# Linear attention on one core: how the rows of two late output stores are dealt to DMA queues and engines

## The chip, the cores and the metric

The kernel runs on one core of a Trainium2 chip. The time is the device time of one execution in microseconds. The profile is one execution recorded by the hardware; its engines are PE (matmul; PEld its weight loads), DVE, ACT (ScalarE), POOL and SP, which issues DMAs, beside 16 DMA engines that move the data.

## The reference

Linear attention with the feature map elu + 1, for 32 heads, 2048 positions and 128 features in bf16:

```python
phi_q = jnp.where(q > 0, q + 1, jnp.exp(q)) + 1e-6
phi_k = jnp.where(k > 0, k + 1, jnp.exp(k)) + 1e-6
kv = jnp.einsum("bhsd,bhse->bhde", phi_k, v)
z = jnp.einsum("bhsd->bhd", phi_k)
num = jnp.einsum("bhqd,bhde->bhqe", phi_q, kv)
den = jnp.einsum("bhqd,bhd->bhq", phi_q, z)[..., None] + 1e-6
return num / den
```

Each head reads three arrays of 512 KB and writes one of 512 KB.

## The kernel before

A head is one unit of work. Its 2048 positions lie 16 to a partition, so a head of k, v, q or of the output is 128 rows of 4096 contiguous bytes, one row for each partition. For each head:

- SP issues three loads (L361) into a ring of six buffers.
- ACT takes exp of k (L368), DVE takes min(exp, 1) + eps (L382), POOL takes relu of k (L372) and adds both for some of the tiles (L390).
- PE accumulates phi_k times (1, v) in PSUM (L413); ACT copies the result to `kvs_sb` (L430).
- PE transposes q (L436); ACT takes exp of it (L447) and relu of one half (L454), DVE relu of the other half (L456) and min(exp, 1) + eps (L468).
- PE multiplies by `kvs_sb` (L483, L484); DVE takes denominators (L506), reciprocals (L512) and the products that are the output (L517, L524). For the last two heads ACT does some of these products (L536).
- SP issues the store (L571) from a ring of ten output buffers `o_sb`.

The order is written by hand. Every operation is added to a plan with an engine and a key (`pl.add`), and each engine runs its operations in order of their keys; the plan derives the semaphore waits from what an operation reads and writes. A DMA is issued by the engine in whose order it stands, and each engine that issues DMAs has a queue of its own. Loads have keys some six heads ahead; a store's key is `late = h + 1.0 + 0.18 * h`, so the stores fall behind the loads and the last ones come after all loads. Before the change all loads and stores are on SP's queue; ACT issues one DMA of 64 bytes at the very start.

A store adds to a semaphore of its slot: `bo`, the output buffer's number, for all heads, and slot `NBO` for the second part of the last head. At the end SP waits for all of them (L226).

`PARTS` (L252) names heads whose store is cut by partitions. Before the change it cuts head 29 (`LAST - 2`) into 51, 13 and 64 rows, all from SP, one behind the other. Head 30 goes out whole, head 31 in two parts by columns (2304 and 1792 bytes of each row).

On ACT the keys around the change are 29.05 for the copy of head 30's sums (L430), 29.9 for the exp of head 31's q (L447), the last exp of the kernel, and 30.0 for its relu (L454).

Of the kernel before, what the change touches and what calls it, by code (L numbers as in the profile page):

```python
# [7 lines left out]
P = 128  # L8
# [223 lines left out]
def bass_standalone__linear_attn_elu__prompt_kernel(  # L232
# [6 lines left out]
    B, H, S, D = q.shape  # L239
    assert D == P and S == 16 * P  # L240
    NT = 16
# [3 lines left out]
    NBI = 6  # L245
    NBO = 10
# [2 lines left out]
    NG = 7  # L249
    HALF = NT * P // 2  # L250
    LAST = NH - 1
    PARTS = {LAST - 2: (51, 13, 64)}  # L252

    ADD = (10, 11, 12, 13, 14)
    EVEN, ODD = tuple(range(0, NT, 2)), tuple(range(1, NT, 2))
# [7 lines left out]
    of = out.rearrange("b h s d -> (b h) s d")  # L263

    with ExitStack() as es:
        def sb(name, shape, dt):
            return es.enter_context(nc.sbuf_tensor(name, shape, dt))
# [13 lines left out]
        o_sb = sb("o_sb", [P, NBO, NT, D], bf16)  # L281
# [12 lines left out]
        def dma_sem(name):  # L294
            return dsems[name]

        for n, c in (("k", NBI), ("q", NBI), ("v", NBI), ("va", 1), ("o", NBO + 1)):
            for i in range(c):
                dsems[(n, i)] = es.enter_context(nc.semaphore(f"s_{n}{i}"))

        pl = Plan()

        def rows(x, h):
            return x[h].rearrange("(p j) d -> p (j d)", j=NT)
# [46 lines left out]
        for h in range(NH):  # L351
# [3 lines left out]
            bi, b2, b3, bo = h % NBI, h % 2, h % 3, h % NBO  # L355
# [211 lines left out]
                last_tile(h + 0.925)  # L567
                div(4, 5, h + 0.93)

            def store(t0, t1, key, parts, slot, p0=0, p1=P, h=h, bo=bo):  # L570
                pl.add("sp", key, lambda sp: sp.dma_start(rows(of, h)[p0:p1, t0 * D:t1 * D],  # L571
                                                          o_sb[p0:p1, bo, t0:t1].rearrange("p j d -> p (j d)")),
                       reads=[("o", bo, p) for p in parts], dma=("o", slot))

            late = h + 1.0 + 0.18 * h
            if h < LAST:
                p0 = 0
                for n in PARTS.get(h, (P,)):
                    store(0, NT, late, ("t", 0, 1, 2, 3, 4), bo, p0, p0 + n)
                    p0 += n  # L580
                assert p0 == P
            else:
                store(0, 9, late, (0, 1, 2), bo)
                store(9, NT, late + 0.01, (3, 4, "t"), NBO)
# [30 lines left out]
```

## Time and profile before

| | us |
|---|---|
| median of three runs (lowest, highest) | 168.23 (168.01, 168.49) |
| the profiled execution, its own time | 167.82 |
| its span | 166.5 |
| busy: PE, DVE, ACT, POOL | 156.0, 152.3, 155.0, 106.3 |
| DMA: 67.25 MB | mean 404 GB/s |
| SP's final wait for stores, in total | 3.0 |

The span runs from the first to the last recorded instruction; the time of an execution has some 1.3 us more around it. Busy times overlap, since engines work side by side: three engines over 90% busy do not say which one sets the end. For this, one reads the chain of waits back from the end, and near the end what the DMA engines still have to move. "To landing" is the time from the issue of a transfer until the last of its DMA engines has reported.

### The profile page before, as it was taken

The page shows a single profiled execution, that of the slowest core. Times are in us where ns is not written, and L with a number is a line of the kernel's source. Part 1 is how long each engine was busy: PE and PEld are TensorE (multiplying, and loading weights), DVE is VectorE, ACT ScalarE, POOL GpSimd, SP SyncE. Part 2 cuts the span into 40 slices and gives each one's busy share as a digit, 9 for nine tenths or more (in the row PEclk, how much of TensorE's full clock was granted, in tenths as well). Part 3 has the DMA queues.
Part 4 walks back from the last instruction along what each step waited for, and adds up shares of the span by engine and source line. Part 5 has one row for each costly group of instructions (what it writes and reads, how often), then busy time and mean ns, then how long its engine had stood idle before and what let it go on. Part 6 is the DMA issues. An engine that isn't in the chain of part 4 may idle for free.

```text
span 166.5 us, 6269 instructions
## 1 busy us (share of the span) xinstructions
PE 156.0 (94%) x2819; PEld 145.3 (87%) x2453; DVE 152.3 (91%) x270; ACT 155.0 (93%) x143; POOL 106.3 (64%) x128
## 2 busy tenths in 40 slices
PE   7789999999999999999999999999999999999960
PEld 0259999999999999899999989999998999999950
DVE  0587999999999999999999999999999999999991
ACT  3979999999999999999999999999999999998790
POOL 2405788676767877676778867676787767677300
PEclk9999999999999999999999999999999999999998
DMA  5999999999999999999999999999999999999986
GB/s 205 345 417 421 413 415 419 412 407 418 417 416 419 422 417 417 422 421 411 424 420 414 423 421 415 419 421 415 422 420 416 422 421 418 418 421 418 415 310 239
DMA packets 18605, 67.25 MB, mean 404 GB/s; under 512 B 2082, under 2 KB 2210, under 8 KB 18594
## 3 DMA queue, kind: packets, MB, share of 16 engines
q1 hardware_dynamic: 18592, 67.12, 99.4%
q8 instruction: 5, 0.08, 0.2%
q14 instruction: 6, 0.05, 0.1%
q10 hardware_dynamic: 2, 0.00, 0.0%
HBM read 50.33 MB, written 16.78 MB: 403 GB/s over the span
## 4 chain that ended last, share of the span: by engine, by line
DVE 58%; PE 17%; POOL 12%; ACT 6%; issue 3%; DMA 2%; DVEq 0%
DVE o_sb L524 20%; POOL rk_sb L390 12%; DVE rq_sb L456 11%; DVE emk_sb L382 10%; DVE emq_sb L468 9%; PE kvz_ps L413 6%; PE o_ps L483 5%; PE o_ps L484 5%; ACT ek_sb L368 3%; DVE rden_sb L512 3%; DVE o_sb L517 3%; ACT eq_sb L447 2%; DMA k_sb<-in_k_dram 2%; DVE den_sb L506 2%; DVE rk_sb L390 1%
## 5 line engine op out<-in xcount | busy, mean ns | idle before, releaser
L413 PE MATMUL kvz_ps<-v_sb,rk_sb 128*128 128x129 bf16 (+1 forms) x512 | 67.0, 220 | 2.8 <-DVE rk_sb L390 1.0
L524 DVE TENSOR_TENSOR o_sb<-o_ps,rden_sb 128x768 bf16<-128x768 f32 (+2 forms) x62 | 67.8, 1135 | 0.0
L390 POOL TENSOR_TENSOR rk_sb<-rk_sb,emk_sb 128x640 bf16<-128x640 bf16 x30 | 41.9, 1395 | 39.5 <-DVE emq_sb L468 38.2
L372 POOL TENSOR_SCALAR rk_sb<-k_sb 128x1024 bf16<-128x1024 bf16 (+1 forms) x60 | 64.1, 1068 | 2.5 <-DMA k_sb<-in_k_dram 2.5
L483 PE MATMUL o_ps<-kvs_sb,emq_sb 128*128 128x129 bf16 (+1 forms) x536 | 65.2, 217 | 0.0
L484 PE MATMUL o_ps<-kvs_sb,rq_sb 128*128 128x129 bf16 (+1 forms) x536 | 64.4, 217 | 0.0
L368 ACT ACTIVATE ek_sb<-k_sb 128x2048 bf16<-128x2048 bf16 x32 | 61.0, 1907 | 2.6 <-DMA k_sb<-in_k_dram 2.6
L447 ACT ACTIVATE eq_sb<-xT_ps 128x2048 bf16<-128x2048 bf16 (+1 forms) x33 | 60.0, 1821 | 2.0 <-PE xT_ps L436 2.0
L413 PE MATMUL kvz_ps<-v_sb,emk_sb 128*128 128x129 bf16 (+1 forms) x338 | 53.3, 221 | 0.6 <-DVE emk_sb L382 0.3
L413 PEld LDWEIGHTS kvz_ps<-v_sb,rk_sb 128*128 128x128 bf16 x512 | 46.1, 98 | 7.6 <-POOL rk_sb L390 2.7
L483 PEld LDWEIGHTS o_ps<-kvs_sb,emq_sb 128*128 128x128 bf16 x536 | 51.2, 98 | 0.8 <-issue 0.3
L484 PEld LDWEIGHTS o_ps<-kvs_sb,rq_sb 128*128 128x128 bf16 x536 | 51.3, 98 | 0.0
L436 PE MATMUL xT_ps<-ident,q_sb 128*128 128x128 bf16 x512 | 33.8, 219 | 0.6 <-DMA q_sb<-in_q_dram 0.4
L436 PEld LDWEIGHTS xT_ps<-ident,q_sb 128*128 128x128 bf16 x512 | 29.9, 98 | 5.1 <-DMA q_sb<-in_q_dram 4.2
L413 PEld LDWEIGHTS kvz_ps<-v_sb,emk_sb 128*128 128x128 bf16 x338 | 32.5, 98 | 0.9 <-DVE emk_sb L382 0.5
L320 PE MATMUL kvz_ps<-ones_sb,rk_sb 128*128 128x1 bf16 x232 | 31.3, 165 | 0.0
L454 ACT ACTIVATE rq_sb<-xT_ps 128x1024 bf16<-128x1024 bf16 x30 | 30.9, 1029 | 0.0
L382 DVE TENSOR_SCALAR emk_sb<-ek_sb 128x2048 bf16<-128x2048 bf16 x32 | 22.0, 688 | 5.6 <-ACT ek_sb L368 5.6
L456 DVE TENSOR_SCALAR rq_sb<-xT_ps 128x1024 bf16<-128x1024 bf16 x34 | 23.3, 690 | 1.1 <-PE o_ps L484 1.0
L468 DVE TENSOR_SCALAR emq_sb<-eq_sb 128x2048 bf16<-128x2048 bf16 x32 | 22.1, 690 | 0.0
L320 PE MATMUL kvz_ps<-ones_sb,emk_sb 128*128 128x1 bf16 x121 | 19.9, 166 | 0.0
L430 ACT ACTIVATE kvs_sb<-kvz_ps 128x129 bf16<-128x129 f32 x32 | 9.0, 281 | 1.6 <-PE kvz_ps L413 0.9
(28 smaller groups left out, 49.2 us busy)
## 6 DMA issues: line engine op xcount, KB each, us to landing
k_sb<-in_k_dram SPq DMA_DIRECT2D x32, 512.0 KB, 15.0
q_sb<-in_q_dram SPq DMA_DIRECT2D x32, 512.0 KB, 15.1
v_sb<-in_v_dram SPq DMA_DIRECT2D x32, 512.0 KB, 15.1
out_dram<-o_sb SPq DMA_DIRECT2D x30, 512.0 KB, 15.3
out_dram<-o_sb SPq DMA_DIRECT2D x1, 288.0 KB, 3.7
out_dram<-o_sb SPq DMA_DIRECT2D x1, 256.0 KB
out_dram<-o_sb SPq DMA_DIRECT2D x1, 224.0 KB, 3.6
out_dram<-o_sb SPq DMA_DIRECT2D x1, 204.0 KB
```

The source lines that it names most:

```text
L320: return pe.add_instruction(mybir.InstMatmult(start_tensor_calc=start, stop_tensor_calc=stop, ldweights=False, bass_skip_group_check=True, ...
L368: lambda a, bi=bi, b2=b2: a.activation(ek_sb[:, b2, :], k_sb[:, bi, :], ACT.Exp),
L372: pl.add(eng, key, lambda e: e.tensor_scalar(rk_sb[:, b3, c], k_sb[:, bi, c], BIG, 0.0, op0=ALU.min, op1=ALU.max), reads=[("k", bi)] + ([( ...
L382: lambda d, b2=b2, b3=b3: d.tensor_scalar(emk_sb[:, b3, :], ek_sb[:, b2, :], 1.0, EPS, op0=ALU.min, op1=ALU.add),
L390: return e.tensor_tensor(out=a, in0=a, in1=b, op=ALU.add)
L413: last = pe.matmul(kvz_ps[:, 1 - l:NC], lhsT=w, rhs=v_sb[:, bi, c - l:c + D], start=first, stop=fin, skip_group_check=True)
L436: last = pe.transpose(xT_ps[:, j * P:(j + 1) * P], q_sb[:, bi, j * P:(j + 1) * P], ident[:])
L447: halves[part] = pl.add("act", key, lambda a: a.activation(eq_sb[:, b2, c], xT_ps[:, c], ACT.Exp), reads=both[part:part + 1] or both, writ ...
L456: f = lambda d: d.tensor_scalar(rq_sb[:, b3, c], xT_ps[:, c], 0.0, None, op0=ALU.max)
L483: pe.matmul(o_ap, lhsT=emq_sb[:, b3, t * P:(t + 1) * P], rhs=kvs_sb[:, b3, c0:c1], start=True, stop=False)
L484: return pe.matmul(o_ap, lhsT=rq_sb[:, b3, t * P:(t + 1) * P], rhs=kvs_sb[:, b3, c0:c1], start=False, stop=True)
L524: pl.add("dve", key, lambda d: d.tensor_tensor(out=o_sb[:, bo, 3 * g0:3 * g1, :].rearrange("p (a b) d -> p a b d", b=3), in0=_ap(full, bas ...
```

## The change

Head 29 goes out in one transfer of 128 rows. Head 28's store is cut instead: rows 0 to 59 from SP, at the place of the old store, and rows 60 to 127 from ACT, with the key `LAST - 1.5` = 29.5, which puts the issue between the copy at 29.05 and the exp at 29.9. The part on ACT has a semaphore slot of its own, `NBO + 1`.

```diff
-    PARTS = {LAST - 2: (51, 13, 64)}
+    PARTS = {LAST - 3: (("sp", 60), ("act", 68))}
...
-        for n, c in (("k", NBI), ("q", NBI), ("v", NBI), ("va", 1), ("o", NBO + 1)):
+        for n, c in (("k", NBI), ("q", NBI), ("v", NBI), ("va", 1), ("o", NBO + 2)):
...
-            def store(t0, t1, key, parts, slot, p0=0, p1=P, h=h, bo=bo):
-                pl.add("sp", key, lambda sp: sp.dma_start(rows(of, h)[p0:p1, t0 * D:t1 * D],
-                                                          o_sb[p0:p1, bo, t0:t1].rearrange("p j d -> p (j d)")),
+            def store(t0, t1, key, parts, slot, p0=0, p1=P, eng="sp", h=h, bo=bo):
+                pl.add(eng, key if eng == "sp" else LAST - 1.5, lambda e: e.dma_start(rows(of, h)[p0:p1, t0 * D:t1 * D],
+                                                       o_sb[p0:p1, bo, t0:t1].rearrange("p j d -> p (j d)")),
                        reads=[("o", bo, p) for p in parts], dma=("o", slot))
...
-                for n in PARTS.get(h, (P,)):
-                    store(0, NT, late, ("t", 0, 1, 2, 3, 4), bo, p0, p0 + n)
+                for eng, n in PARTS.get(h, (("sp", P),)):
+                    store(0, NT, late, ("t", 0, 1, 2, 3, 4), bo if eng == "sp" else NBO + 1, p0, p0 + n, eng)
```

## The prediction

> **What bounds the kernel now.** I read the page first, then the last entries of the chain of waits, then the DMA share in windows over the end, then the trace's own records of DMA packets and landings (one landing for each DMA engine that carries a part of a transfer). From the page:
>
> ```profile
> span 166.5 us, 6269 instructions
> ...
> DMA  5999999999999999999999999999999999999986
> ...
> out_dram<-o_sb SPq DMA_DIRECT2D x1, 288.0 KB, 3.7
> out_dram<-o_sb SPq DMA_DIRECT2D x1, 256.0 KB
> out_dram<-o_sb SPq DMA_DIRECT2D x1, 224.0 KB, 3.6
> ```
>
> The DMA engines are nearly full from start to end, and the last store, 224 KB, takes 3.6 us from issue to landing. The chain of waits ends with compute, at 162.84 us:
>
> ```profile
> 162.18 0.20 DVE o_sb L517
> 162.37 0.47 DVE o_sb L524
> ```
>
> The span ends at 166.53. So the last 3.6 us are this store's, and the question is whether they are the latency of a transfer or a backlog. The windows answer (columns: stretch, its length, busy us of PE, PEld, DVE, ACT, POOL, granted clock, DMA share, GB/s):
>
> ```profile
> 158.00:160.00 2.00, 1.91 (x37) 1.74 (x35) 1.89 (x6) 1.83 (x8) 0.00 (x0) 1.00 1.01 363
> 160.00:162.00 2.00, 1.08 (x20) 0.90 (x16) 1.90 (x8) 1.90 (x8) 0.00 (x0) 1.00 0.67 248
> ...
> 164.00:165.00 1.00, 0.00 (x0) 0.00 (x0) 0.00 (x0) 0.00 (x0) 0.00 (x0) 1.00 0.70 276
> 165.00:166.00 1.00, 0.00 (x0) 0.00 (x0) 0.00 (x0) 0.00 (x0) 0.00 (x0) 0.78 0.24 93
> ```
>
> Between 160 and 162 us a third of the DMA engines stand idle, and in the last full microsecond only a quarter work: some engines have a backlog, others none. The same in landings. Head 28's store was issued at 152.48; its 16 engines landed at 159.06 to 159.43 (eight of them, called early), then 160.45 (A), 160.51 (B), 160.78 (C), 161.26 and 161.28 (D, E), 161.58 (F), 161.69 (G) and 163.08 (S). The view of DMA issues for that window gives the slowest:
>
> ```profile
> out_dram<-o_sb SPq DMA_DIRECT2D x1, 512.0 KB, 10.6
> ```
>
> The very last store landed on ten engines by 164.94 and on the others at 165.42, 165.74, 165.97, 166.37, 166.42 and 166.48. **The end is the backlog of the most loaded DMA engine**; without any the span would end near 164.95, so at most 1.55 us can be won.
>
> **How rows become a time.** A row (4096 bytes, one partition) takes 0.156 us on an engine. Of a whole store each engine has 8 rows, 1.25 us, which is also the step between an engine's landings from head to head; only S is slower, 1.32 us (0.165 a row) from head 27 to 28. Head 29's slot shows how pieces are dealt: two increments right after the issues of the small pieces, then 32 landings, which is 3 + 13 + 16 for 51, 13 and 64 rows. So a piece goes to as many engines as the largest number up to 16 that divides its rows. A landed head 28 at 160.45, and a landing follows at 163.09, 17 rows later; B likewise at 163.15. So A and B are two of the three with 17 + 1 + 4 = 22 rows of head 29; the third is early. All others had 5 or 4 rows. Of the eight early engines four land the 13-row piece at 159.39 to 159.55, one is the third of the three, and three have no such landing. So the ten between the three and the last three are four early engines and C to S.
>
> Check of the model: A 160.45 + 22 x 0.156 = 163.88 (landed 163.86); S 163.08 + 5 x 0.176 = 163.96 (as landed). From there heads 30 and 31 take all late engines 2.52 us (163.96 to 166.48). A, B and S thus end within 0.11 us of each other: the end has three holders.
>
> **The change part by part.** It deals the same 256 rows of heads 28 and 29 out otherwise. By the rule seen in the counts, 60 rows go to 15 engines with 4 each and 68 to 4 engines with 17 each; I take these to be the lowest-numbered, as the 3 and the 13 nest. Head 29 then gives 8 to each. With t an engine's landing of head 28 in this trace:
> - The three of before (A, B, an early one): 8 + 22 = 30 rows become 4 + 17 + 8 = 29. A ends at 160.45 + 21 x 0.156 + 2.52 = 166.25, B at 166.31.
> - An engine with only the 4-row piece: 12 rows for 13. S, if it is one: 163.96 - 0.17 + 2.52 = 166.31.
> - **The fourth engine**, which had 13 rows, now has 29: it ends at t + 21 x 0.156 + 2.52 = t + 5.80. An early one: 165.2, no matter. C: 166.58. D or E: 167.07. F: 167.38. G: 167.49. S: 163.08 + 21 x 0.17 + 2.52 = 169.2.
>
> The Trainium skill ("DMA: Bandwidth & Descriptors", Why a DMA increments its semaphore by 16) states the same dealing, the largest k up to 16 that divides the slowest dimension, on the lowest-numbered engines; the counts 3, 13 and 16 agree, and its figure leaves the sum as it is.
>
> - **ScalarE's issue.** It stands between the copy to kvs and head 31's exp, and the timeline of ACT has room there:
>
> ```profile
> 153.16 0.28 ACT L430 ACTIVATE kvs_sb<-kvz_ps 128x129 bf16<-128x129 f32 x1
> 155.07 1.88 ACT L447 ACTIVATE eq_sb<-xT_ps 128x2048 bf16<-128x2048 bf16 x1 [1.63 <-PE xT_ps L436]
> ```
>
>  Head 28's last division ends at 152.45, before ACT arrives at 153.44, so the issue does not wait. SP's issues of stores take 0.32 to 0.55 us here with a short queue, 2.9 us with a long one. ACT's queue is empty, so I take 0.4 us, hidden by the 1.63 us wait for PE; at 2.9 us exp would be 1.3 us late, and DVE's chain after it.
> - **A second queue.** The 17 rows no longer stand behind heads 26 and 27 on their engines. That changes the order, not the sum of rows. Whether an engine loses time while it serves two queues the trace shows only for instruction fetches: after the 16 KB one at 37.6 us (0.94 us) one engine was 1.5 us further behind. Ends: no gain or loss, up to some 0.5 us; I take none, since 4 KB rows keep 0.156 us wherever they follow each other.
> - **SP** issues head 29 in one piece for three, 0.32 + 0.55 us less in a queue that then waits for the engines anyway until head 30's output is whole (160.94). Nothing.
>
> So the sum hangs on which engine is the fourth. By count it is one of ten: early 4, C 1, D or E 2, F or G 2, S 1. One more sign: the 64-row piece found six idle early engines, whose first packets start at 159.13, 159.19, 159.21, 159.26, 159.28 and 159.32. If packets are handed out in engine order, with the last two among engines 13 to 15, the step is about 0.019 us and the first of the six would be about engine 5; an early fourth engine would start near 159.09, where nothing starts afresh. I halve the early engines' chance for it and raise that of D to G.
>
> The Trainium skill (same page, Latency and other measured facts) says that DMA engines 7 and 15 are usually the slower ones; the trace has one slow engine and it is not among the last three, so 7 would fit, and by that S would not be the fourth. I give it the count's chance, a little reduced, from the step above alone.
>
> **The forecast and its rivals.** Profiled execution: 167.82 us, a span of 166.53 and 1.30 around it. The median of the runs shown, 168.23, is 0.41 above it; I add differences of span to the median.
> - Forecast: the fourth engine is one of D to G and becomes the end, +0.59, +0.90 or +1.01, in the middle +0.8: **169.0** (own range 168.7 to 169.35). For it: seven of sixteen engines lag, and the start order. Chance 0.55.
> - Rival 1, the other side: the fourth is early, the three holders each give up one row: 166.31 for 166.48, -0.17: 168.06. It decides as long as the fourth lands head 28 before 160.5. Against it: the start order. Chance 0.2. If it is C: +0.1, 168.33, chance 0.1. A gain of over 0.3% would need more than 0.5 us, which no holder gives up.
> - Rival 2: the fourth is S: +2.7, 170.9. Chance 0.07.
> - Rival 3, the change does not do what it says: the 128 rows of head 28 spread evenly after all, 8 to each engine. S then carries 163.08 + 8 x 0.165 + 2.52 = 166.92, +0.44: 168.67. Chance 0.04. The Trainium skill (same page, Rules for kernel authors) says just that of two transfers to disjoint halves: they share the same 16 engines, so one should not bother. The counts of head 29 speak against an even spread.
> - Rival 4: the second queue or a long issue on ACT costs 0.5 to 1.3 us, 168.7 to 169.5. Chance 0.04.
>
> The range from 168.0 to 169.4 holds all but S, the far end of rival 4 and some scatter below 168.06. A change under 0.3%, 0.5 us, can hardly be told from none here (the three runs span 0.48 us). Faster by more: 0.03. Within: rival 1, C, rival 3 and a third of D and E, 0.39. Slower by more: 0.58.
>
> **What would show it.** Right: head 28 with 15 + 4 landings; head 29's last landing near 164.5 to 165.0 on one engine alone, while A, B and S land it near 163.75; a last window with the DMA share of one engine (0.06). Wrong, rival 1: head 29 complete by 163.8 and the last store's landing under 3.5 us after issue. Wrong otherwise: exp at L447 later than 155.07, or rows of over 0.16 us while two queues are served.

## The result and the profile after

| | before | after |
|---|---|---|
| median of 8 runs each, us | 168.03 | 168.74 |
| ratio, 95% interval | | 1.0046 (1.0027 to 1.0065) |
| profiled execution, own time and span, us | 167.82, 166.5 | 168.82, 167.5 |
| end of the chain of waits, us | 162.84 | 162.51 |
| last store, issue to last landing, us | 3.6 | 4.9 |

The kernel became slower by 0.46%, 0.7 to 0.8 us. Compute ended 0.33 us earlier in the profile after; the loss is all in the stores behind it. The page after, its DMA issues (engine that issues, count, KB, us to landing):

```profile
out_dram<-o_sb SPq DMA_DIRECT2D x1, 288.0 KB, 5.1
out_dram<-o_sb ACTq DMA_DIRECT2D x1, 272.0 KB
out_dram<-o_sb SPq DMA_DIRECT2D x1, 240.0 KB, 11.6
out_dram<-o_sb SPq DMA_DIRECT2D x1, 224.0 KB, 4.9
```

Neither of the last two stores changed, yet both take 1.3 to 1.4 us longer. The chain of waits after ends where it did, on DVE:

```profile
161.85 0.20 DVE o_sb L517
162.04 0.47 DVE o_sb L524
```

and the windows of the profile after (the last two columns are DMA share and GB/s) show what comes behind:

```profile
164.00:165.00 1.00, 0.00 (x0) 0.00 (x0) 0.00 (x0) 0.00 (x0) 0.00 (x0) 0.50 0.39 151
165.00:166.00 1.00, 0.00 (x0) 0.00 (x0) 0.00 (x0) 0.00 (x0) 0.00 (x0) 0.50 0.12 48
166.00:167.00 1.00, 0.00 (x0) 0.00 (x0) 0.00 (x0) 0.00 (x0) 0.00 (x0) 0.50 0.07 26
```

One engine of sixteen is a share of 0.0625. In the last full microsecond hardly more than one DMA engine works, and none of the compute engines does. The landings agree: the last store landed on eleven engines by 164.61, then at 164.96, 165.33, 165.48, 166.29 and 167.48. Before, the last three lay within 0.11 us of each other (166.37 to 166.48); now one engine ends 1.19 us behind all others.

Nothing is to be seen of a wait on ScalarE. Its timeline after has the issue, 0.28 us, beside the copy, and exp waits for PE exactly as long as before:

```profile
152.83 0.28 ACT L430 ACTIVATE kvs_sb<-kvz_ps 128x129 bf16<-128x129 f32 x1
152.84 0.28 ACTq L571 DMA_DIRECT2D out_dram<-o_sb  x1
154.74 1.88 ACT L447 ACTIVATE eq_sb<-xT_ps 128x2048 bf16<-128x2048 bf16 x1 [1.63 <-PE xT_ps L436]
```

### The profile page after: what moved, and what is told of

It is laid out like the page before. It is cut to its first block, busy times and chain, and to the rows that moved or that the text cites. A ratio compares the mean times of both kernels' runs of the same rounds, so it can differ in the third digit from the quotient of the medians.

```text
span 167.5 us, 6268 instructions
## 1 busy us (share of the span) xinstructions
PE 156.2 (93%) x2819; PEld 145.7 (87%) x2453; DVE 152.1 (91%) x270; ACT 155.0 (93%) x143; POOL 106.4 (64%) x128
## 4 chain that ended last, share of the span: by engine, by line
DVE 58%; PE 17%; POOL 12%; ACT 6%; issue 2%; DMA 2%; DVEq 0%
DVE o_sb L524 20%; POOL rk_sb L390 12%; DVE rq_sb L456 11%; DVE emk_sb L382 9%; DVE emq_sb L468 9%; PE kvz_ps L413 6%; PE o_ps L483 5%; PE o_ps L484 5%; ACT ek_sb L368 3%; DVE rden_sb L512 3%; DVE o_sb L517 3%; ACT eq_sb L447 2%; DMA k_sb<-in_k_dram 2%; DVE den_sb L506 2%; DVE rk_sb L390 1%
```

## The experiments

The theory, of the deal: rows are dealt to engines by the size of a piece alone, and the fourth engine, which lags, now has 29 rows after head 27 for 13. The rival, of the queue: the second queue or its issue costs. All kernels below are the changed kernel with another `PARTS`, except for the map; ratios are against the kernel before, run on the same chip.

**e1, the same pieces from one queue.**

```diff
-    PARTS = {LAST - 3: (("sp", 60), ("act", 68))}
+    PARTS = {LAST - 3: (("sp", 60), ("sp", 68))}
```

> Head 28 is cut into the same 60 and 68 rows, but both pieces leave from SP's queue, and ScalarE issues none. Theory of the deal (the fourth DMA engine gets 29 rows and ends alone, whatever queue they come from): as the changed kernel, +0.5 to +0.9 us over the kernel before. Rival of the queue (what costs is the second queue, or the issue on ScalarE): back within 0.2 us of the kernel before.

Measured: 168.92 us, 1.0063 (1.0038 to 1.0088). By the medians that is 1.05 us over the kernel before, a little above the 0.5 to 0.9 expected; the interval holds 0.64 to 1.48 us. The loss is there without any issue of this store from ScalarE. The windows of this kernel end as those after:

```profile
165.00:166.00 1.00, 0.00 (x0) 0.00 (x0) 0.00 (x0) 0.00 (x0) 0.00 (x0) 0.86 0.14 53
166.00:167.00 1.00, 0.00 (x0) 0.00 (x0) 0.00 (x0) 0.00 (x0) 0.00 (x0) 0.50 0.07 26
```

One engine ends at 167.45, alone, the next one at 166.27. Its packets can be followed in the trace, since on a busy engine each starts within some ns of the end of the one before. It landed head 27 at 159.70 or 159.71 (two engines land there) and finished its 4 of the 60 rows at 159.98, but its 17 of the 68 rows only at 163.27, 3.30 us later, where 17 rows of 0.156 us make 2.65. Between the 13th and the 14th of these rows stands an instruction fetch; the next part comes back to it. The engine that lagged most beside the slow one (head 24 at 156.63) is not the one that ends last. It had none of the 68 rows: it landed its 4 rows at 161.02 and head 29, 8 rows later, at 162.25.

**e2, the second queue with the old deal.**

```diff
-    PARTS = {LAST - 3: (("sp", 60), ("act", 68))}
+    PARTS = {LAST - 3: (("act", 51), ("sp", 13), ("sp", 64))}
```

> Head 28 is cut as head 29 was before the change, 51, 13 and 64 rows, with the 51 from ScalarE's queue; head 29 goes out whole. The three lowest engines have 30 rows after head 27 and the fourth has 13 again, as before the change. Theory of the deal: -0.1 to +0.2 us against the kernel before. Rival of the queue: still +0.5 to +0.9 us, since 51 of the 68 rows still come from the second queue.

Measured: 167.97 us, 0.9998 (0.9981 to 1.0014). 51 rows still come from ScalarE's queue, and the loss is gone. e1 and e2 together rule out the rival as the cause of the loss: the pieces cost, not the queue.

**e3, more rows for the same four.**

```diff
-    PARTS = {LAST - 3: (("sp", 60), ("act", 68))}
+    PARTS = {LAST - 3: (("sp", 36), ("act", 92))}
```

> ScalarE's piece has 92 rows instead of 68, SP's 36 instead of 60: 23 rows to each of four engines and 3 to each of twelve. The four have 34 rows after head 27 instead of 29. Theory of the deal: 5 rows of 0.156 us, +0.8 us more than the changed kernel, +1.3 to +1.7 us over the kernel before. Rival of the queue as an issue or a fixed cost: no more than the changed kernel, within 0.2 us of it.

Measured: 169.38 us, 1.0105 (1.0075 to 1.0136), 1.5 us over the kernel before on its chip, against 0.7 to 0.8 for the change. Five more rows at 0.156 us are 0.78 us. By the medians the step from the change is about that (0.80). From e1, on the same chip, it is 0.46, and between the last landings of the two profiles 0.47 (167.48 and 167.95), so the direction is shown and the size only roughly. In the profile one engine ends alone at 167.95, the next at 166.20.

**e4, a map of the engines.** Head 27 goes out as 15/16 of its columns whole, and the first 128 columns in small pieces (the part of the edit that does it; the rest gives the pieces their semaphores and leaves out head 27's usual store):

```diff
+                if h == LAST - 4:
+                    store(1, NT, late, ("t", 0, 1, 2, 3, 4), bo)
+                    for i, n in enumerate(tuple(range(1, 16)) + (8,)):
+                        store(0, 1, late, ("t", 0, 1, 2, 3, 4), NBO + 2 + i, p0, p0 + n)
+                        p0 += n
```

> The changed kernel, with head 27's store in two sorts of pieces: columns 128 to 2047 whole, and the first 128 columns (256 bytes of each row) in pieces of 1, 2, 3 and so on to 15 and 8 rows, each with a semaphore of its own, so that the piece of n rows tells which DMA engine is which. Theory of the deal: the piece of 4 rows has a landing more than 1 us behind those of 1 to 3 rows or beside a late one, and the slow engine of 0.17 us a row appears only in a piece of more than 4 rows. If the piece of 4 rows adds an early engine, the fourth engine did not make the end and the theory falls.

Measured (landings from the trace, us; a piece of n rows has n of them):

| piece | landings | the engine it adds |
|---|---|---|
| 1 row | 159.35 | first: 159.35 |
| 2 rows | 159.68, 160.53 | second: 160.53 |
| 3 rows | 160.01, 160.69, 160.86 | third: 160.69 |
| 4 rows | 160.62, 161.01, 161.21, 163.28 | **fourth: 163.28** |
| 5 rows | 160.98, 161.36, 161.38, 162.31, 163.45 | fifth: 162.31 |
| 6 rows | 159.83, then five as above | sixth: 159.83 |

From one piece to the next, engines come up at about the same place a little later, so a new place is the new engine. The fourth engine is the last of all, by 2 us behind the first three, which carry 17 rows from ScalarE as it does. The fifth is the slow one: it landed head 24 1.55 us behind any other (157.94), and its head 27 at 162.07 follows in steps of 1.38 us on average, where others take 1.25. Of the sixth to the tenth, two are early and three late (159.2 to 159.9). The fifteenth is late too: the piece of 15 rows adds a landing at 160.25. It landed head 24 2.28 us behind the earliest, more than any other but the slow one. The rest are early, near 158.2. This kernel's own time, 170.39, says nothing, since its pieces add rows to the low engines.

**e5, no cut at all.**

```diff
-    PARTS = {LAST - 3: (("sp", 60), ("act", 68))}
+    PARTS = {}
```

> Heads 28 and 29 both go out whole, 16 rows to each engine. Theory of the deal: the slow engine, with 16 rows after head 27 for 13 before the change, is the end alone: 3 rows of 0.17 us, +0.3 to +0.6 us over the kernel before, and the next engine, the fourth, ends over 1 us earlier. If the slow engine were no holder of the end before the change: no slower than the kernel before.

Measured: 168.33 us, 1.0022 (1.0009 to 1.0036), at the lower end of what was expected. The profile's span is 166.9. The slow engine landed head 28 at 163.12 and ended at 166.90; the next at 165.50. In the windows there is half an engine's microsecond left behind 166:

```profile
165.00:166.00 1.00, 0.00 (x0) 0.00 (x0) 0.00 (x0) 0.00 (x0) 0.00 (x0) 0.79 0.07 26
166.00:167.00 1.00, 0.00 (x0) 0.00 (x0) 0.00 (x0) 0.00 (x0) 0.00 (x0) 0.50 0.03 11
```

So the slow engine is a holder of the end, and cutting is worth 0.2% by taking rows off it. The change's cut came out worse than none (0.46% against 0.22%, though the intervals overlap).

**e6, rows for the slow engine.**

```diff
-    PARTS = {LAST - 3: (("sp", 60), ("act", 68))}
+    PARTS = {LAST - 3: (("sp", 32), ("sp", 11), ("act", 85))}
```

> Head 28 goes out as 32 and 11 rows from SP and 85 from ScalarE: by the dealing rule 85 rows are 17 on each of five engines, so the fifth engine now has 2 + 1 + 17 + 8 = 28 rows after head 27 and the fourth the same. By the map of the run before, the fifth engine is the slow one (0.17 us a row, head 27 landed near 161.8). Theory of the deal with that map: 161.8 + 28 x 0.17 + 2.5 = 169.1 as the end of the span, +2 to +2.7 us over the kernel before. If the slow engine is another than the fifth: as the changed kernel, +0.5 to +1.0 us.

Measured: 170.2 us, 1.0144 (1.0122 to 1.0166), +2.3 us; the span's end is 168.88 for the 169.1 expected. The windows of this kernel have two engines at work from 166 us and one from 167:

```profile
166.00:167.00 1.00, 0.00 (x0) 0.00 (x0) 0.00 (x0) 0.00 (x0) 0.00 (x0) 0.50 0.12 48
167.00:168.00 1.00, 0.00 (x0) 0.00 (x0) 0.00 (x0) 0.00 (x0) 0.00 (x0) 0.50 0.07 26
```

They are the slow fifth engine (168.88) and the fourth (167.34). It shows both the dealing rule for 85 rows and the fifth place of the slow engine.

No deal tried beats the kernel before. That no other cut would is not shown.

## Why the prediction was right

- **What bounds the kernel.** Right. The end is the most loaded DMA engine; compute ended 0.33 us earlier and the span 1.00 us later.
- **The deal.** Right. Head 28's slots show 15 and 4 landings, and e6 shows five engines for 85 rows. That the lowest engines get them was assumed; the map, where engines join in a fixed order, agrees.
- **The slow engine** gives up a row: 166.31 predicted, 166.29 measured.
- **The fourth engine.** Right that it lags and ends alone: after, head 29 lands last at 165.01 on one engine, the next at 163.79. The predicted ends of D to G were 167.07 to 167.49; measured were 167.48 after and 167.45 in e1. That these agree so well is luck: two things that the sum did not have cancel, as the next two points show.
- **Its lag was smaller.** The engine was less late than D to G. At head 24 those four stood 2.2 to 2.7 us behind the earliest. Followed by its packets, the engine that ends last stood 1.8 to 1.9 us behind after, in e1 and in the map, nearer to C (1.74). With these lags the prediction's formula gives an end of 166.8 after and in e1.
- **An instruction fetch falls on it.** The DMA engines also carry these; the profile after has two from 155 us on, of 16 and 8 KB (queue, kind: packets, MB, share of 16 engines):

```profile
q8 instruction: 1, 0.02, 0.4%
q14 instruction: 1, 0.01, 0.1%
```

The second one takes 0.31 us from 161.418, right behind the last of ScalarE's rows on this engine; in e1 it starts at 162.001, behind the 13th of the 17 rows. In both the next two rows take 0.37 and 0.31 us instead of 0.156. Together this costs 0.65 us and accounts for the 0.64 to 0.70 us between 166.8 and the measured ends. The prediction put nothing for it. It named instruction fetches, but only with a view to two queues and by the 16 KB one at 37.6 us; the profile before has this 8 KB fetch too, at 161.978, with slow rows of 0.37 and 0.30 us behind it. There it follows the rows of F or G, on an engine with one of the 13 rows and none of the 51. So F or G may have been the fourth in that execution, which is not shown.

No run moves the fetch, so its share of the loss is an estimate: without its 0.65 us this engine would end near 166.83, 0.35 us later than the end before (166.48), where the profile shows 1.00.

- **A and B** do not bear out as steady holders. After, the other three of the four ended at 164.96 to 165.48 where 166.25 and 166.31 were predicted: the lags of the lowest three were smaller in that execution. Lags differ from one execution to the next, and a profile shows one.
- **The start order** of packets gave the right answer for the fourth engine by a partly wrong reading. It had put an early engine at the fifth index; the map, in its own execution, has the late sixth engine there and early ones at the eighth and ninth places.
- **The slow engine's number.** The Trainium skill ("DMA: Bandwidth & Descriptors", Latency and other measured facts) names engines 7 and 15, counted from 0, as usually slower. Here the slow one is the fifth, number 4, by the map and by e6; the measurement decides.
- **ScalarE's issue** was put at 0.4 us, hidden; it took 0.28 us and was hidden. **The second queue** at nothing: 68 rows at 0.159 us each, and e2 within 0.2% of the kernel before.
- **Size.** +0.8 us predicted, +0.71 between the medians; by the points on the lag and the fetch, this closeness is partly luck. The time itself, 169.0, is 0.26 us high, most of it since the three runs first shown were 0.2 us above the median of eight.

## What to carry to other kernels

Where the DMA engines are full to the end, a transfer ends with its latest engine, so look at the landings of single engines and not at the mean share. Cutting a store by partitions deals its rows by divisibility (51 to 3 engines, 68 to 4, 60 to 15), in these runs from the first engine on; a cut can pay only if the engines that gain rows are early enough. Find out which ones lag with pieces of 1, 2, 3 rows, each on its own semaphore, before choosing a cut. Tell engines apart by the rows that they carry and not by their lag alone: in the map, the engine with the largest lag but one is the fifteenth, which carries none of ScalarE's rows.

## What was not expected of the hardware

- ScalarE's queue was empty, and still its first packet started at 156.38, 3.5 us after the issue at 152.84; in e2, e3 and e6 it was 3.4 to 3.5 us too. SP's 13-row piece, in the profile before, landed its first row 1.8 us after its issue.
- From there an engine with both queues takes one row from each in turn: ScalarE's rows on one engine start mostly every 0.31 us, each recorded as 0.159 us long. The Trainium skill (same page, Rules for kernel authors) says that spreading DMAs over issuing engines brings no bandwidth, since they share the same 16 engines; e1 beside the changed kernel agrees, in that the second queue brings no gain clear of the noise (1.0063, 1.0038 to 1.0088, without it; 1.0046, 1.0027 to 1.0065, with it).
- The slow engine is slow in stores: while only stores run, it takes about 1.38 us (1.36 to 1.40 in the profile before) for its 8 rows of a head where the others take 1.25.
- An 8 KB instruction fetch costs one DMA engine more than its own 0.31 us: in the seven profiles where that engine had rows left, the next row took 0.34 to 0.37 us and the one after 0.30 to 0.32.
